# Second products of scores and key bits contracted over the rows in use, and no clearing of the other rows, in a fused LSH attention and two-layer MoE kernel

## The chip, the cores and the metric

The kernel runs on one core of a Trainium2 chip. The metric is the device time of one execution in microseconds (us). Five engines work side by side: TensorE (PE, with its weight loads shown apart as PEld), VectorE (DVE), ScalarE (ACT), GpSimd (POOL) and SyncE (SP), which here only issues DMAs. Each engine runs its instructions in the order in which they were written for it.

## What is computed

```python
q_bits = (einsum('bhsd,dk->bhsk', q, proj) > 0)      # 6 bits per row, B=2 H=8 S=768 D=64
k_bits = (einsum('bhsd,dk->bhsk', k, proj) > 0)
mask   = bucket(q_bits)[:, :, :, None] == bucket(k_bits)[:, :, None, :]
scores = where(mask, q @ k.T / sqrt(D), -1e9)
attn   = softmax(scores)                             # row sum + 1e-9
x      = (attn @ v) as [1536, 512]
h = x @ w_in;   g = piecewise(h);    x = g @ w_out   # 512 -> 2048 -> 512
h = x @ w_in2;  g = h - tanh(h);     out = g @ w_out2
```

Everything is wanted in float32 accuracy, so nearly every product is made of three: high part by high part, high by low and low by high.

## The kernel before, in words

The attention is cut into 32 groups (batch, pair of heads, half of the queries, head of the pair), and each group into three tiles of 128 queries by 768 keys: 96 tiles. Batch 0 comes first (48 tiles); the matmuls of the two MoE layers of batch 0 are mixed between the tiles of batch 1, and those of batch 1 come at the end, on other, 16-bit parts.

For a group, `prep_q` and `prep_k` split the queries and keys. A key tile has two halves of storage: `a` (128 partitions, high part twice over) and `b_`, in which partitions 0 to 63 hold the low part and partitions 64 to 75 (`R0:RC`, twelve rows) the hash bits of the keys. The queries have `Aq` and `Bq` in the same way. Scores of a tile are two products into one PSUM tile (`emit_s`): `first` contracts `Aq` with `a` over 128 partitions, `second` contracts `Bq` with `b_` over 128 partitions, twice each since the 768 keys are two halves of 384. A mismatch of bits adds a large number, so a minimum over the row (L662) and an exponential (L663) give the softmax.

The bits come from a product too. `first_k` (for the first two heads) and `k_bits` (for all others) make, for each half of 384 keys, two matmuls into the one bank `pb`: `phl_w` with `a`, and `phz` with `b_` (L419, L436), both over 128 partitions. VectorE then compares `pb` with a threshold and writes the twelve bit rows of `b_` (L422, L439). `q_bits` does the same for the queries with other weights (L449, L450, L453).

Partitions 76 to 127 of `b_` and `Bq` are in no use. Since the products run over 128 partitions they must hold zeros: POOL clears two key tiles (L284) and three query tiles (L293) at the start, one DVE memset clears a piece of `phz` (L304), and `prep_k` calls `clear` (L395 to L402) for each of the six other key tiles of batch 0, which live in storage that the MoE uses later. The key tiles of batch 1 reuse the first two, so nothing is cleared there.

The order of all this work is not found by the program while it runs: each operation is entered in a plan with the engines that could do it, and `SCHEDULE` is a packed list that gives the order of all operations and the engine of each (`Plan.unpack`). 64 entries of the plan are fillers (`spin`, L1330): four small matmuls each whose result nobody reads.

Of the kernel before, what the change touches and what calls it, by code (L numbers as in the profile page):

```python
# [23 lines left out]
    "c-rk)X^dUvd4At-|IWVLbMC(1xifQTyLUW`XT~$0@q)+L#s<d;F<>xz0!eAv9B@zqA*3mVqAHM84lxb1P)JLnhEigcAGD;XRU`7F66)_rRi*yupQ>uw12*<7"  # L24
    "_l`{h5>ow2ckY~XzvbPY=Y7A=00ELK{?1w9oCEqc1@nKt_VVICzANOB5lfL5if_C@NQ#Bw3ml1!fg~tU4y2!Ck_-OCtpQei>zT8HB>VIjo;X2O#!Nu~p(#9c"
    "H@WxVknJHjECU*=$_3|h$KMrlyGP3R-Yc?bPv()ajEr;5rbI~Qg5e4v5~O*lPY<0I>e8L;CU23mJ$!Bf0SPERH@6iRcfj}p1t6bnqdj{W9I#+{`ikA=vWYkL"
    "<Dk{X1=^1iw+&RVJYD7W*;2EPwNkAFg%adTBLIs-t;%37J3Ct}<=X8+!5YSNI#V1QX$@ssne>1Ww_$8-Y$R&MgK?<>&8VPK;g+xxUK_@RMm4U5g~C{51%+&w"
    "d+(FUgqSzIY#vYLa+xUOrZDvY6kq;?@-3@sWy?_|lL3=z-v~fO@N~njyWeFtSiqco{xRnX%PLwHp;>1cxk#JvyV1*c2>m4&P1~g2gl8jphA`qPt}IKPkN`JU"
    "QYru6{urdsge%13dl=qt*vz!p<xJkSP2z67br}}g_u-Z;WKrlvs)kyVM`rj87jWg39Y`EVk&^?a&7Nz0o0#9c)a1r9`wr}@a~1y~{m!00C{yt@@i^kcVvaqy"
    "z`yiWHot|y)O}wjTE9xh2_?txwcF&*J6|M!KKwaKDIvmo&JyI7r%u+mCj5HA9_Noe^c499d4iDNNA?JN8-MZeL44yO_SRSMp(~I)@aARW0r3j{@2@%D|C3Yf"  # L30
    "$3OlXln%mO|9PkWcU%Gu&pvzoZNCEf+}kIm1MoxZouMCmAO7X%C%$+1djKZBj{2!nn!ZN0rmraLuYUHrGU-qL3t92kIQt`-f05>L&%ellJx3A^AEVJTt{?98"
    "e{~oAHhkxo@BA`&`|V&XLI^#>r10jO|N0Ma>0kV_P3i_AipV&AgTT*TMMTGYjR3`0_)pEdj1U>Zi!Ld^^DYDXS<auKCr_TVjn7yo@Ptm30nT$;FFuy@v*^Vv"
    "k{~QW4f>F6T8`s{4twPI7wqHSOlSw?;O>ClX3)<IMY%)y*ZJWTKYFbZa5m_%{gPd0-@;r9G(qY%!zIo^pv#hN7TUxeWM^JG4zYLHwz3Y*DRW}_)`?F|9HKWE"
    "$xvdcQ93fxCY`MvI=^jxNV#fj|K`nfc9x5onYz|f)k$NSl-1be9yL}TEpalWXK_UJDLSz<7;mn3GOW_rd_>Upe0m~1SQseKE1GgV>WmL{cI;?`G;C!08e1xr"
    "TBbT}c_Lk)ol-nSGZO{dZn=Y+sA#mGT+)a2`E6lPpABki&ex-|Fh1NVmxG2e(irvqD;kxoQI)QdiJVl_?}RxVEMm1;;O;c?$$rKLW1FR`+blL?`tBC9gyTqp"
    "$)k2wTsLmklyx|0Uuic(Lfiv&&*YBQR=6B8COs`vCKh?j4P&#MPN##yCRb}22vZFyt{1H|<wl*(gqeB0Wh$6_-7FMM9fpUp7BYEYaCk7<+oDu1D<R!#^?}$t"
    "?vSOWV`$#9RW01HAm?5A4QKk+>0AFO{dE=DH*TVTuNC7*9)9?X?kSWnk;6){;7|2^{uln~Pjp_oPyhU_yP31k{JZbkru>mE3Q(`zkb70(TT+VX(Z6`(FO8IC"
    "h}RDr`jpOyXKmZg*)M!0dw*6~U<%RaUE=+<?eWa*H`*_&*fw5LW+wRNpP8`&tsU*1^7P+IcFdNZP{vP{4onR%xyw&j&ubxnc=Mxb``zjXdg*>wM^uT=GWH}t"
    "#vEp!ypdVof0S#k_3i#u`bqZSx4tEWWh-IY_uqFtKYEm3_i)vGh;up2B|bRDIm>#i?!vLXG)3_aeC&30+vl;F|BU?P&9^99+=5>oxZX6y@nc7iAitN$;4bNW"
    "8g1kOvis0IAn(ahNlVurp`d@y`E>X@oTR14Zs2^`u3wfEk|~)0<Fh*{qIVPB->00t*FtE|UbRdBb{fX^@D97exHmtbHnE$*F3@X_`e2S<eRUrrap5qtfDQsn"  # L40
    "*va1CmSgSqUNSbe-AA4t8p7J_owF)RxNyc<c6JHmJJb!OQNzYzsW!<Sdb=@g95U>Ka=$dQ3IbW&y>)rlXe2&0EVAywLoSWe4$M#<R(zWB!VJxlB|@$cxdWkj"
    "v~$hX`#K#}QpH-Vt)R4|gH}-3TaZm3^iCMjY|#o9l<&HI?tU{3me}OSozUEtTB3f?G8~wl%}Gbi&`EP@!5oscrP`6JY}YsRoPBWi69plfEj^LlGi42BEYUIN"
    "%7(83p%f{#+g?%`YBj-a1y0Lz28!<Wg)!;W!Oobr4Fxp}N(iCsg0gB+Suhsl%iO_CJ8wE8x?`u%>JTOQNMpM)mi)!RKEL5_617f^lgouzwq$W|hb$DA%A0v("
    "xG_;0V9kRE+q|03=XVb6;H<nWE;Sd*t-h-c=CNLY%L)f4NtD|kRd!WiCq{X{oe%x~m{Pp09!-%ZX$1adCE|r6*PyvvxNTQbC31(1n{;}9UwTU;iu?Ndrgp>_"
    "ZOW))y1k{ayikafXu=e12NA^mm$zpR4#=@D;+_#}FB=-4bo}ZzbCj`b9Ou%J;YDYQ-mK@Ke>yYWmr)(nR(sl)LMqi6Nq4T?K9rV&a{KNh3(EtoDUc%A)f8f4"
    "OzabjrYMb$8s-e*P`jNQRtjeZT1`DR(9{i`s_S7(6DZYMNvQ#z%Vl$%vM7$za3D+flK%emZpg;<u$EBL!X^H~Yzo4C#jR5d(}Vz`H9fs`W}yu*AHjIiQPqNx"
    ">Tm#N?2U!_sqw!4z5&u8MeWxMWs<8CxwTmVUCE~7Vq7d0a!YYBmm9G(#*m5nGSOt*mrAj6TaJp6mhZcxZi^+Z8w{O#8KO#5XXSi47o{L$I_b0-$NM6WhF%c#"
    "kN9q1z3y4_RnT=SE)|O<8nxRc4RSOyGpsTyHf3tqXw*|uw)`MarRr{ZN&ONjwJw+>tx|JQCKV+FE2KHKsWaK>2;UgRQQI-O*)mEXl~F4t$}3&06rF-%32dYx"
    "BQGaaBU#U3t|+mBQQ#ViTE*$u4FW#TZ9%2WsXbvjR?-QLQz@EEByNrdQgMljTAAi4%jZMaqmdWs8M{esYp71CYuQcTsvBq-m8wxnn`VK;EH{=RL0ZbeWH{%("
    "?enBED{9$!+Xw=dBANzD1yLY(GV0UNQIjSkv!>A|wWN_Qmy#AaX=X`Zj>nQyPHCC=9*GJGxjB}dYN0bQFz8sO=hf>LRBJW2!pmiDdKw^M-8jel1qTu+%PrS^"  # L50
    "m$-Qlm{2`Wx+m~t()~Cbu>d5eAW4$sL&av`Q^|KK$&#eh!7v75a2Q>}`jW1=X?o_BWku|Qw5)7VW-=zRmj`Sx9D;7uQ2c$V%DK8sLD7`|?F(-rX9*1{`X9b2"
    "JItqyS(d|07^F#OuB+K(YsP4*l%kL)B|<XAAWiIaWQy1`TsLV+h|MHeRmU<=8~wVRfFkb_#TarLg;p52EoIKQNhsP5MU#{akdVVH2qkz_6lKP8kkot+NDA!G"
    "noQXcSf(R}pkocXMk^_6jYfY%*P-6$S-M=OIm+|gk=a}(n>aLbSST%7XReXx;w71o1B9Z4D4m2(#nb>d>7fz_C!HNln!$b`nWSZfupC0bec#W6mrbU`c3_7o"
    "@HSyG!I&_T6OC&R^xMT&KiEdYs%DKwxuQ!9O2w#<ph)F%(n!-GKZ$C;fua_<)Cq!OkT(sBo4ItHg($HKI3cs13kCv}1`g=a#04=#f`%+eamW(CNN7ZeDU!&m"
    "K>JO{%BhNzDVc5oWR6;eETl8OOnet6{$^-XYJv;NAuqv?<S1Agy@YrucqFN!iJeK>AiBtsUO8!BDTu^+#snmRg|mWSpA}dk1XjFy_W`;IS@C!ELN;`nL)Ncw"
    "ZkHZgtRKB{;Ho(nus~NGJ|w}9Xzcl>UHHp)-{Nnp!^d3kBXa$3D~4fwcx(0ef7O!#7v-XSTu^sWE+)jqbh{`Q<>M^med!Lhi?I9uO6IsG_P9D7$VZVHxGv|&"
    "*)M$WPNZ8-;;PZf6TuD6fA~Ra%egJdnS&JhfHi83No2$G+ls^5ihT&4i^&?jV4bnBE^uq!pZj^E1LFrhQ=Qg=thN?cMg@BwOUVTtY~PP<53_y))>@NJ>)nD~"
    "R>h5O7VwPoaN|hy&=c4BbM*#YgN_$s^9O?}Suu&My*xPgg5YXEU~e2F_P|bW2b>*@U1Eb5Y*?=?Pb-f-VS~7#p65-rwV@}c>5KHh?73+KdniqMQY5ZbVl9V|"
    "b(?gVaoW#hrT*B14iPsd&0YkuY74|w>TCea)wA*Z-abRJq*t)8H;C7(LV6&hy93BN=0NPqdbpNqx?j|t$y4m^GhD+G2&;nF1((>1<FR*D=;k1@zF^=+1$4FR"
# [1320 lines left out]
```

## Time and profile before

| | us |
|---|---|
| three runs, median | 725.91 |
| lowest and highest of them | 722.04, 726.06 |
| the profiled execution | 722.02 |
| its span (first to last instruction) | 720.2 |
| around the span | 1.8 |

The profile is that of the fourth execution, which is 3.9 us below the median of the three. Every row in this document comes from it. PE and PEld are busy times whose ends are modelled, so a share near 100% says that matmuls follow one another, not that each is as fast as can be. The chain of work is followed back from the last instruction: at each step to what released it, or to the instruction before it on its engine.

### The profile page before, as it was taken

What the parts mean: (1) busy time and instruction counts of PE and PEld (TensorE: products, weight loads), DVE (VectorE), ACT (ScalarE), POOL (GpSimd) and SP (SyncE); (2) the same over time, 40 slices, a digit from 0 to 9 for tenths busy, and PEclk for the clock granted to TensorE, in tenths of its full rate; (3) what the DMA queues carried; (4) which work ended last, traced back from release to release, by engine and by line L of the source; (5) the groups of instructions that cost most, each with busy time, mean ns of one, the idle gap of its engine ahead of it and who ended that gap; (6) DMA issues with size and microseconds to landing.
All of it is one profiled execution on the core that took longest, in us unless ns stands there. A gap on an engine that the chain in (4) does not pass through costs nothing.

```text
span 720.2 us, 12689 instructions
## 1 busy us (share of the span) xinstructions
PE 698.8 (97%) x4516; PEld 558.1 (77%) x4516; DVE 645.4 (90%) x973; ACT 506.3 (70%) x852; POOL 464.4 (64%) x383
## 2 busy tenths in 40 slices
...
GB/s 238 209 219 303 250 303 291 232 214 247 259 250 259 214 277 229 188 255 253 186 182 227 230 256 155 196 118 82 107 63 103 59 78 28 100 59 88 45 45 87
DMA packets 168655, 129.45 MB, mean 180 GB/s; under 512 B 127840, under 2 KB 138640, under 8 KB 168592
## 3 DMA queue, kind: packets, MB, share of 16 engines
...
## 4 chain that ended last, share of the span: by engine, by line
PE 75%; DVE 16%; issue 3%; DMA 3%; ACT 2%; POOL 0%; SPq 0%; DVEq 0%; ACTq 0%
PE mm L1043 44%; PE sbk L1076 8%; PE pv L1076 4%; PE pv L771 3%; PE ss L644 3%; PE ss L648 3%; DVE smt L662 3%; PE pb L1076 2%; PE pv L761 2%; DMA pt<-phl 1%; DVE phl L668 1%; PE sbk L1031 1%; DMA krs<-in_kT 1%; DVE wr L941 1%; PE mm L731 1%
## 5 line engine op out<-in xcount | busy, mean ns | idle before, releaser
L1043 PEld LDWEIGHTS <-late_w 128*128 128x128 f16 x720 | 70.4, 98 | 48.8 <-issue 2.2
L663 ACT ACTIVATE p<-ss,smt 128x768 f32<-128x768 f32 x78 | 70.1, 898 | 53.9 <-DVE smt L662 52.1
L670 POOL TENSOR_TENSOR phl<-p,phl 128x768 f16<-128x768 f32 x44 | 77.0, 1750 | 40.3 <-ACT phl L668 15.2
L662 DVE TENSOR_REDUCE smt<-ss 128x1 f32<-128x770 f32 x82 | 78.3, 955 | 15.1 <-PE ss L648 12.9
L1043 PE MATMUL mm<-late_gh,late_w 128*128 128x384 f16 x368 | 85.5, 326 | 2.0 <-DVE accs L1168 2.0
L963 POOL TENSOR_TENSOR wl<-wr,wh 128x512 fp32r<-128x512 f32 x49 | 69.6, 1427 | 25.4 <-DVE wh L961 11.3
L1076 PEld LDWEIGHTS <-late_w 128*128 128x128 f16 x528 | 51.1, 98 | 35.4 <-issue 2.4
L1043 PE MATMUL mm<-xh,wh 128*128 128x384 f32 x256 | 72.1, 342 | 1.8 <-DVE tmp L1145 1.7
L1043 PE MATMUL mm<-gh,wh 128*128 128x384 f32 x256 | 72.5, 343 | 0.6 <-DVE accs L1179 0.6
L1043 PE MATMUL mm<-xh,wl 128*128 128x384 f32 x256 | 70.7, 337 | 0.0
L1043 PE MATMUL mm<-gh,wl 128*128 128x384 f32 x256 | 70.6, 336 | 0.0
L1043 PE MATMUL mm<-xl,wh 128*128 128x384 f32 x256 | 70.5, 336 | 0.0
L1043 PE MATMUL mm<-gl,wh 128*128 128x384 f32 x256 | 70.4, 336 | 0.0
L963 POOL TENSOR_TENSOR late_w<-wr,late_w 128x512 f16<-128x512 f32 x34 | 46.1, 1360 | 14.8 <-ACT late_w L961 12.5
L962 POOL CAST wh<-wr 128x512 fp32r<-128x512 f32 x34 | 26.9, 795 | 38.1 <-PE mm L1043 22.1
L1043 PEld LDWEIGHTS mm<-xh,wh 128*128 128x128 f32 x256 | 46.3, 188 | 5.2 <-DVE tmp L1145 2.4
L941 DVE SCALAR_TENSOR_TENSOR wr<-w,wr 128x512 int32<-128x512 int32 x64 | 49.3, 782 | 1.0 <-ACT wr L939 0.2
L1043 PEld LDWEIGHTS mm<-gh,wh 128*128 128x128 f32 x256 | 46.3, 188 | 2.7 <-issue 1.7
L1043 PEld LDWEIGHTS mm<-xh,wl 128*128 128x128 f32 x256 | 46.9, 188 | 0.0
L1043 PEld LDWEIGHTS mm<-gh,wl 128*128 128x128 f32 x256 | 46.8, 188 | 0.0
L1043 PEld LDWEIGHTS mm<-xl,wh 128*128 128x128 f32 x256 | 46.8, 188 | 0.0
L1043 PEld LDWEIGHTS mm<-gl,wh 128*128 128x128 f32 x256 | 46.7, 188 | 0.0
...
## 6 DMA issues: line engine op xcount, KB each, us to landing
...
```

Source lines behind the costliest of these rows:

```text
L644: T.matmul(ps[:, c, 0:SH], Aq[n][:, i * 128:(i + 1) * 128], a[:, c * SH:(c + 1) * SH], start=True, stop=False)
L648: T.matmul(ps[:, c, 0:SH], Bq[n][:, i * 128:(i + 1) * 128], b_[:, c * SH:(c + 1) * SH], start=False, stop=True)
L662: one("V", 870.0, lambda: V.tensor_reduce(z, sx, axis=AX.XY, op=ALU.min), cell, [c])
L663: one("A", 880.0, lambda: A.activation(halves(p), s, AF.Exp, bias=z, scale=-1.0, accum_out=LS[lm][:, lk:lk + 1]), cell + [c], pc + [("ls", ...
L670: lo = [("G", 1600.0, lambda: G.tensor_tensor(hl[:, S:2 * S], p, hl[:, 0:S], op=ALU.subtract)), ("V", 870.0, lambda: V.tensor_tensor(hl[:, ...
L761: T.matmul(ps[j * 64:j * 64 + 64], f[:, kc, j, :], pt[j][:, kc, 0:SH + 1], start=kc == 0, stop=kc == KC - 1)
L771: T.matmul(ps[j * 64:j * 64 + 64], v[:, kc, a, j, :], PT[n[j]][:, c * KC + kc, 0:SH + 1], start=(kc == 0 and i == 0), stop=(kc == KC - 1 a ...
L941: one("V", 600.0, lambda: V.scalar_tensor_tensor(wi, yi, 3, wi, op0=ALU.logical_shift_left, op1=ALU.bitwise_or), [("w64", i, 0)], [("wr", ...
L962: ("G", 580.0, lambda: G.tensor_copy(whl(n)[0], WR[r]))], [("wr", r)], [("wh", n)])
L963: op([("G", 1225.0, lambda: G.tensor_tensor(whl(n)[1], WR[r], full(whl(n)[0]), op=ALU.subtract)), ("V", 600.0, lambda: V.tensor_tensor(whl ...
L1043: T.matmul(ps[:, s + hf, 0:SH], m[:, kc * 128:(kc + 1) * 128], y[:, hf * SH:(hf + 1) * SH], start=(kc == 0 and i == 0), stop=(kc == 3 and ...
L1076: T.matmul(sbk(n), m[:, sl], v, start=(j == 0 and i == 0), stop=(j == 1 and i == 2))
```

## The change

The second product of the scores runs over 76 partitions in place of 128 (`Bq[n][0:RC]`, `b_[0:RC]`), and the second product of the keys' bits over 64 (`phz[0:R0]`, `b_[0:R0]`). All the clearing is gone: the memsets at L284, L293 and L304, the function `clear` and its six calls. The bits' product is no longer entered as a reader of the bit rows. `SCHEDULE` is packed anew. Unpacked as `Plan.unpack` does it, the list has 3,614 operations in place of 3,620: the six clears (four on ACT, two on POOL) are gone, all others but the fillers stand in the old order and on the old engines, and four of the 64 fillers stand later, from within the first 206 places of the list to places 211 to 213 and 995.

```diff
-    for m in range(2):
-        G.memset(Bk[m][R0:].bitcast(F32), 0.0)
...
-    for z in Bq:
-        G.memset(z[R0:].bitcast(F32), 0.0)
...
-    V.memset(phz[64:128, R0:RC].bitcast(F32), 0.0)
...
         a, b_, ac, bc = kt(g)
-        if b == 0:
-            clear(b_, bc[1:3])
         m2 = kcount[b, hp, j] % len(kr)
...
-    def clear(t, cells):
-
-        n = t.shape[-1]
-        src = warm[R0:].unsqueeze(1).to_broadcast([R0, n // 128, 128])
-        dst = t[R0:].rearrange("p (a b) -> p a b", b=128)
-        op([("A", 100.0 + n * 0.82, lambda: A.activation(dst, src, AF.Copy, scale=0.0)),
-            ("V", 60.0 + n * 1.04, lambda: V.memset(t[R0:].bitcast(F32), 0.0), 1),
-            ("G", 60.0 + n * 0.8, lambda: G.memset(t[R0:].bitcast(F32), 0.0))], [], cells)
...
                 T.matmul(ps, phl_w, a[:, cols], start=True, stop=False)
-                T.matmul(ps, phz, b_[:, cols], start=False, stop=True)
-
-            one("PE", 350.0, mk, [ac[c], lo] + bc[1 + c:2 + c], ["pb"])
+                T.matmul(ps, phz[0:R0], b_[0:R0, cols], start=False, stop=True)
+
+            one("PE", 350.0, mk, [ac[c], lo], ["pb"])
...
                 T.matmul(ps, phl_w, a[:, cols], start=True, stop=False)
-                T.matmul(ps, phz, b_[:, cols], start=False, stop=True)
-
-            one("PE", 350.0, mk, ac + bc[0:1] + bc[1 + c:2 + c], ["pb"])
+                T.matmul(ps, phz[0:R0], b_[0:R0, cols], start=False, stop=True)
+
+            one("PE", 350.0, mk, ac + bc[0:1], ["pb"])
...
-                T.matmul(ps[:, c, 0:SH], Bq[n][:, i * 128:(i + 1) * 128], b_[:, c * SH:(c + 1) * SH], start=False, stop=True)
+                T.matmul(ps[:, c, 0:SH], Bq[n][0:RC, i * 128:(i + 1) * 128], b_[0:RC, c * SH:(c + 1) * SH], start=False, stop=True)
```

## Rows read from the trace of the kernel before

**Rows 1.** The page: busy time of each engine, share of the span, instructions.

```profile
PE 698.8 (97%) x4516; PEld 558.1 (77%) x4516; DVE 645.4 (90%) x973; ACT 506.3 (70%) x852; POOL 464.4 (64%) x383
```

**Rows 2.** The page: the chain that ended last, by engine.

```profile
PE 75%; DVE 16%; issue 3%; DMA 3%; ACT 2%; POOL 0%; SPq 0%; DVEq 0%; ACTq 0%
```

**Rows 3.** Busy time by stretch: us, PE, PEld, DVE, ACT, POOL, PEclk, DMA share, GB/s.

```profile
24.00:48.00 24.00, 19.89 (x159) 14.59 (x160) 22.68 (x36) 19.48 (x34) 19.13 (x14) 1.00 1.06 226
156.00:286.00 130.00, 129.34 (x808) 122.51 (x807) 119.99 (x177) 97.31 (x164) 83.00 (x67) 1.00 1.00 247
```

**Rows 4.** The chain in order of time, first 75 us: start, us, what.

```profile
8.24 0.43 POOL xl L402
...
19.36 0.44 PE pb L435
...
61.43 0.18 PE pb L435
```

**Rows 5.** The chain in order of time, from 150 us on.

```profile
173.16 0.18 PE pb L435
...
388.47 3.15 PE mm L1043 x18
...
397.54 0.18 PE pb L435
...
528.57 2.92 PE mm L1043 x18
```

**Rows 6.** Clears by line: count, ns (min/median/max), first and last start, form.

```profile
L284 POOL MEMSET bk<- x2: 732/732/733, 0.7 to 1.4; 64x768 f32 x2
L304 DVE MEMSET pw<- x1: 68/68/68, 3.3 to 3.3; 64x12 f32 x1
L400 ACT ACTIVATE xl<-warm x3: 840/840/844, 7.8 to 34.5; 64x768 fp32r<-64x768 f16 x3
L402 POOL MEMSET gl<- x1: 738/738/738, 39.2 to 39.2; 64x768 f32 x1
```

**Rows 7.** Timeline around the clears: start, us, engine, instruction [idle before, releaser].

```profile
5.88 0.99 POOL L340 TENSOR_TENSOR bk<-krs,ak 64x384 fp32r<-64x384 f32 x1 [2.60 <-ACT ak L331]
...
34.49 0.84 ACT L400 ACTIVATE xl<-warm 64x768 fp32r<-64x768 f16 x1
...
36.80 0.90 ACT L663 ACTIVATE p<-mm,smt 128x768 f32<-128x768 f32 x1 [0.45 <-DVE smt L662]
...
41.29 0.19 PEld L449 LDWEIGHTS pb<-ab,pw 128*128 128x128 f32 x1 [0.31 <-POOL ab L340]
```

**Rows 8.** Timeline of PE around a group of matmuls with 64 output columns.

```profile
119.32 0.34 PE L1043 MATMUL mm<-gh,wl 128*128 128x384 f32 x1
119.58 0.88 PE L708 MATMUL pb<-unit,ls 128*64 128x128 f32 x12
120.39 0.44 PE L1043 MATMUL mm<-xh,wh 128*128 128x384 f32 x1
120.67 0.34 PE L1043 MATMUL mm<-xl,wh 128*128 128x384 f32 x1
```

**Rows 9.** Timeline of PEld and PE around a transpose of six columns.

```profile
229.20 0.08 PEld L695 LDWEIGHTS pb<-unit,ls 128*6 128x6 f32 x1
...
229.38 0.27 PE L695 MATMUL pb<-unit,ls 128*6 128x128 f32 x1
229.40 0.59 PE L1043 MATMUL mm<-xh,wh 128*128 128x384 f32 x2
```

**Rows 10.** By line: weight loads of 6 and of 128 columns.

```profile
L695 PEld LDWEIGHTS pb<-unit,ls x8: 81/82/83, 210.0 to 458.9; 128*6 128x6 f32 x8
L648 PEld LDWEIGHTS ss<-bk,ab x112: 186/188/190, 10.7 to 455.6; 128*128 128x128 f32 x112
```

**Rows 11.** Groups by form, first 75 us: form, count | busy us, mean ns | idle.

```profile
L331 ACT ACTIVATE ab<-qr,cb 128x384 fp32r<-128x384 f32 x7 | 4.2, 607 | 0.0
L331 ACT ACTIVATE ab<-qr,cb 64x384 fp32r<-64x384 f32 x2 | 1.2, 608 | 0.0
```

More of the change, by code (lines that the diff above doesn't have):

```diff
@@ L23 @@
 SCHEDULE = (
[L24 to L59, printed above, removed]
@@ L60 @@
-    "HZXl%@{m>QknVt7Q+QUafn9#>Ma`=U?Hcc_ia@vC2)iYD_q4^|=ti2nd%2H*D|$1;(+PqrttRJZdt7PK1r$$Qm2~G}+tZyAcJc6;77h_M>Orul{qL<n&ev^`"
-    "(}+Rn#S}<Z1MK{@gj`@TC94eW5$4_-_U26NmU-**83DTob6q*=+Tw4VE@x8a!fG#`W4H}-3(sW(;@O^J^*Y!Cr?`>l&L9rgyQHVG@5gLy-8q}I>)=b^gBQVd"
-    "dY(B=;rp05|7nD5ylWSaeYo;}XN2W7"
+    "c-rk)X^dUvd4At-|IWVLbMAKTy>qu&?ristXYq_ZV~-a+#x^!~oDc&B0|64#lopeiB`AToX;Wf?qJ%6&gqQ|e8c0i`hEigMAGD-MRU=ZVQq<p(s!ILQAFV2-"
+    "JzyKpa_`tAL5)<u(#)MX_x--_U7z>)jsXHBr~IET2<IHow<(zadFs1wye;I^h^5H0$&U#MSrBj}7)XKw<zV(pOme|b-w|M+Z#{iMkmSel$tS7GnHdNmG=+!m"
@@ new lines @@
+    "gnJJT+a7|$a-gxQTyXBX?`<K+JyJe#Lgdk&EFfc98ReTzi2y!;;RqlSq_Nwh2hRz0=ni(9yM^uMn-&m|fa04r&EwV`FtI>kYHA9|;WpZH`(VEXGY5B@OC}EB"
+    "kk!ToI)D<l4fbJWrpoJc<^DR>%C#~iWhj<M0k#ge`i2Vmxw%rg&~7J*HG<h}t~5T{8qT$H*+C<2!}$34Xw-^_;&LDKM~TXWo5Q~FrZ7$#)wmWW$#`T1Nj@yR"
+    "^OMVkSTwzS5ziJ1xhUsmF!K<UUiyIYEvstfD^XuA2PW0N5rB%|>4sf*pJX;zz?@?7wDY)Sl`M<Uyt9N{WKH<J=%u@b{<MpxZBlR2vynVQ7;zO>mZhGO0JrsJ"
+    "GXB4Q38c@2E5u`a7(QUw%(U3GOrF>#akt*G1Pkr^ar0)fRp_l$4Y#I_&hl9<;JWKN@WD1x<m7;9v*%i0C+1hLHo5W4z61N}T*Y6Y-`MlV6)OHvJcf8mY+?^D"
@@ new lines @@
+    "@K65%o8L@e`u@)ltzRJ%gpvn8X}8He_q;&9JMue}QbL6FoF&K|Pn@Z7P53Q>J;qNz@&x%Zd7O|xLiRcK7XI|qA$<K2_U32tk%LGcdgB`Lka!vY=a(EG_`zBB"
+    "{qO$`N(bS@f83-04HrSfv(Mgg{1+gfd+UsJ0KQ}WeE8enf`9(WQ{O!DO#l;LL;b{AO<$#2)0dU?S3i19ne+$$g{<^TockUvzCa6w=U?E!o+GJ+r)l(z>xX;&"
+    "U!0&{hj0As=RXVHdMg-@5JJx|DZKH<zx@51`ltVBle$5OA~KF&C-9?J5Yh2oB|!0I{zLPG5h6o)!6gYi?=rBT<@_0X=FAz}_^9<1KBZG*fb)XZTTd7KJbE#U"
+    "BnV4TgFa%Lmg6{~!#?-mefERiY-k6S;NE~9H|WQOqTHeU^ZZDLAG^s2I2-cVe#vgO?_e$knl|Y+!zIokpi7c%6xzfcWM@&2I}WjT*|xF{Z&K#u%$<`TnmkNz"
@@ new lines @@
+    "HBwz-sWCb_+9sVX9Xh{leptC`%fQBsbZ(A|+1a|*)72?siB#11)E+fn87p%#tmkl4H5Hv)9EvyAJ2}?Z*mzXX_I!3SJCqD2^kBc7h&mI)ogF(GAq^Y3W@B?-"
+    "UoBUiu{@DYXr~-c)7)fY+bwrU6BUgOkgJ+lpWhY+^|_#?Hu-u?CKDr_N+oC*qm41&KiKHY8&&BVxyZ>x15Q}Lp%Pa66YkC+pBi9nD7IO)y3Jy<rtfYx%Q%4~"
+    "m^x<X#my6DO<6~R_H}lDNQir&?wQ=t+6tFK#-yiZ#>5hjxnXRSGudpAY;d)ffiTsu;(Du<rQE2~*)TV+H%|vsubD~7)M0oyZy}QhhDL^>y)8=Rk`mIbRv(JZ"
+    "2OYAwcoNM|Y*7n$FUWaUe%YD1bLP%3W<ReY`?d}A@3dn4=&4hma?hfCksMKq1%ImV_wW0MKhZ_$KK+w7?`6(D^KYNDP5C`t5};naweX6<H>DKOqkr-GUm6+9"
@@ new lines @@
+    "5U(9E^jVz~&)T+Ku>btC`3LgC0#k^lca`_ow#RdK-Dba}V%vC8nYrMre`dxCw05+2*3&<h?4&I{p^P6Y9he$kbeA5tp4UQt=k`a{_IuU0_2L7rj;InJW9%#Z"
+    "By*U3<~C-1>rt+`)_3{W>#wkfzxFjDEL#cFe&GIF__1UB=2KPk5zgfZm-z5F=Pd8Bx(g@w(hSAB@$_Bl_{Xuo_)+=6+wV}exC1{kc#CO@2TvY5iu{vA1}CKR"
+    "VYHD4$nHn?fc!*(N?N|@C<Xod&WFR_<s>UTb}Q#gcKw=kl1$6AGd{MHB6=U8`<u$ydlQ8A-1SQYV5ebh5AU}7829D})dqGu*a^Mqm=ET}4L39yiIXGD0y+dN"
+    "g(rJ|TaLHed&&6tb{~0mco=JQ_spp%1;bfq$=M~4?@+gv#|#@sq}m{N=<UXgaoDgA$^FvID+pw1_m-tyW0CmKh{(H#4!bnYIxtIl*yq!X7v^Z5ED~~16b^*u"
@@ new lines @@
+    "vCfS*?CW$?S(R$Bwu17a4q8F7H<A55=$$aC*;Xr9P`>Ln-Th`3EV03lJE6HPvq=4*WjHW5SCEdHrBmkgf;lW}i?yTI+pcfuP4=O=4<thLxAbIw&$Kn1vqZ<-"
+    "R55%N2&G85-S*PaP^$@UD{xw#GgxwONyep92RmolHY92Uln_GMiLz=@MKBf=E8M|cyJ$M2x?^Y1>JTOQXk)uF7X7V5O~2u95VcN?lWT=ovSev!hfGR~m5sbH"
+    "(wHm{vi?Jd+PqpU7IzNs;H<JMF841~TFvVZ6|tVcHOZkV5*7AGeY^T#Cq_lTT@3w!m{L4mkETgKX$1Z?W#WaSH=?<e9N(3WiNayyBRV_3FT1%B#m#1OdPj`W"
+    "hMYR7+nbZ6g(Ob13DdA0L=X>L+nzf#D91mAdq%CjY<ObI@vGa+F~)9moU2DiwmO^jM!g9JW^yyloa(5y+S9%oGMUb3wsYO~;jA2z+jk#bSQ>0igA~E8ejz5u"
@@ new lines @@
+    "#Xhms6y>oo!<<DNZnp~~O5yBat6z@~_Uneu)b)s^36yKCbk+bb6!Ha5Sro@vIFP4%$-qE%H{|1bSW6*k;VOS&E(77d(w6Ck8A1Tjnwi-$yU+%hk6<FDRJCBV"
+    "Iud{xd*fkodZIbd93%}=(tbUukV2ivE&Y9<`|{bi6qm|LVKFWh3Zs_B7;;fF7fr>@Oomn3a!ic2eBT{&TPzLTQ0UYv5cNfMRw-r+Q3i6Rlg*lOyf5--=mo*R"
+    "sP8uGb<diwg05R}xl}6CsNF7WkYl;o5tUQ1DKjHRqn?qn<p+T(S9i;+>Q_mrbz+jN%4~{qnJ5KVA<gLxovBVo_{JEH*^bH0mQe<&j9NK0Ug=U_$w?GT+eR8P"
+    "@(NNl()}FfiZV-#gli~i6=!2NWu^1n7F4>N+LNYZrBrBwO3}|m8s=y)6PKx|RcMj2Vli|*8hMePwfm`U4c94kExX^h>IPayU)3mQO*0`eD~#tzkd<;MRp;Ed"
```

13 lines of the change are left out of this document (added).

## The prediction

> **What bounds the kernel now.** I read the page first: PE is busy 698.8 of 720.2 us, DVE 645.4, the others far less [rows 1]. The chain that ended last says the same: 75% PE, 16% DVE [rows 2]. A share is an average, so the next view is the stretches. From 24 to 48 us DVE has 22.7 of 24 us of work and PE 19.9: there PE waits for DVE. From 156 to 286 us PE has 129.3 of 130 [rows 3]. So a microsecond saved on ACT, POOL or DVE in the early part counts only if DVE's queue gets shorter, and one added to PE after about 45 us counts almost everywhere. The granted clock is 1.00 in both stretches [rows 3], the upper of TensorE's two levels; the change leaves the number of matmuls as it is, so I leave the clock out.
>
> In the PE part the pace is set by the weight loads: 18 matmuls of 32-bit parts took 3.15 us, 175 ns each, 18 of the 16-bit parts 2.92 us, 162 ns each, both with 384 columns [rows 5]. The load of a 32-bit part takes 188 ns [rows 10] and runs while the matmul before it streams.
>
> **The clearing that goes.** Four clears on ACT of 0.84 us are 3.4 us; two on POOL and the two of the key tiles at the start are 0.73 each, 2.9 us; the three query tiles are half that size, by estimate 0.37 each, 1.1 us; one DVE memset is 0.07 us [rows 6], where of a line with several tiles one stands and the others are as long. In all 7.5 us of three engines. What lies over it:
>
> At the start POOL, done with its memsets by 3.3 us, sat idle 2.60 us until ACT had split the first keys at 5.88 [rows 7]. The keys' DMA is the cover, and the DVE memset lies under it too. Gain 0. Without that cover it would be the 2.5 us of POOL.
>
> On ACT, the clear at 34.49 has an exponential behind it, and the one after that waits 0.45 us for DVE's minimum at 36.80 all the same [rows 7]. What the clear gives back, ACT spends waiting for DVE, which is full [rows 3]. The two before it, from 7.8 us on [rows 6], lie in the stretch in which the keys still arrive; the fourth is like that at 34.49. Gain 0; all four exposed would be 3.4 us.
>
> On POOL, the clear at 39.2 stands ahead of the subtraction for which a weight load of the queries' bits waits 0.31 us at 41.29 [rows 7]; at most that is won there. The other one, at 8.24, has 0.43 us on the chain [rows 4]; but it lasts 0.73, to 8.97, and the chain leaves it at 8.67, so it did not release what came next. Gain 0, at most 0.7.
>
> So I take 0 for the clears, with 7.5 us as the bound of all of them exposed and about 1 us as the most that the waits show.
>
> **The fillers.** Twelve small matmuls of 128 columns took 0.8 us [rows 8]; the four fillers that move are sixteen of about that size, so about 1.1 us of PE, which is taken from the head and given back later. The bounds are 1.1 us either way; I take 0, since PE waits in both places for others and a filler uses up waiting. No wait is added: the bits' product only loses a reader's entry, and its place stays.
>
> **The second product of the scores, over 76 rows.** Nothing in the trace contracts over fewer than 128 partitions. The nearest rows on the number of partitions are ACT's: the same operation took 607 ns on 128 and 608 on 64 [rows 11]. On PE the load goes with columns: 82 ns for 6, 188 for 128 [rows 10], and here the columns stay 128. So a matmul over 76 rows costs what it cost: 0. The bounds: if the shorter load let these 192 matmuls go at the 16-bit pace, 13 ns each, 2.5 us less; if the array must be emptied ahead of and behind each of the 96 pairs, as below, 96 x 0.38 = 36 us more.
>
> **The second product of the bits, over 64 rows.** There are 16 key tiles with two halves, so 32 such matmuls, each alone between a matmul over 128 rows and another. Here the trace has a near relative: matmuls with 64 output columns, which use half of the array the other way. Around them PE loses time. The last full matmul starts at 119.32, the first narrow one at 119.58: 0.26 us in place of 0.175, so 0.085 lost; the next weight load was not made ahead. Behind the group the first full matmul starts at 120.39 and the second 0.28 later, not 0.175: 0.105 lost, since the first load lay bare [rows 8]. A lone 64-row matmul would pay this on both sides: 0.085 + 0.105 going in, 0.105 + 0.085 coming out, 0.38 us a visit.
>
> The other relative says nothing is lost: the transpose with six columns had its weights loaded at 229.20, ahead of its start at 229.38, and the next matmul starts 0.02 later [rows 9]. I take the first, since it is an ordinary matmul with half an array's 64, and the second a transpose; the bounds are 0 and 0.38 a visit.
>
> A rule of the Trainium skill bears on this. The page TensorEngine Tiling (Array Packing), section Tiling Modes, counts a contraction over 64 rows as a tiling of its own (two tiles of 64 rows), none for 76, and says that changing the tiling mode, not merely the tile, drains TensorE. The 64-column rows agree with it, the six-column ones do not look like a change of mode. By that rule the sum is the one below; by the six-column row alone it would be 722.0.
>
> **The sum.** How many visits lie on the path? The chain holds the bits' matmuls of the keys (L435 and L436 together) six times in the head, the first at 19.36 and the last at 61.43 [rows 4], and nine times from 173.16 to 397.54 [rows 5]: 15 of 32. The other 17 are not in it: the chain passes them on DVE or a DMA, and between 24 and 48 us the bits' comparison would have to wait in DVE's full queue anyway [rows 3]. 15 x 0.38 = 5.7 us more on PE, nothing back from the clears: 720.2 + 5.7 = 725.9 of span, and with 1.8 us around it 727.7. That stands against the profiled execution's 722.0. The runs shown lie at 722.04, 725.91 and 726.06, so two of the four known times are 3.9 us higher; I add half of that, 1.9, and predict 729.6 us. The ratio that I forecast is 727.7 / 722.0, 0.8% slower.
>
> **Rivals.**
> 1. No drain: 64 rows are handled as the six-column transpose was. Then nothing is paid and the clears give back 0 to 1 us: 721 to 722, on the median's scale up to 726. For it: rows 9. Against it: rows 8 are the closer form. Chance 0.20.
> 2. Faster. The weight load gets shorter with its rows, and PE runs at the load's pace where the change acts. Of 192 + 32 matmuls, at 13 ns each, 2.9 us, and with 1 us from the clears 718; it ends over 1% faster only if the clears come free too (7.5 us, 711.6). It decides as soon as a 76-row load falls under the 162 ns of streaming. Against it: ACT's 607 and 608 ns, and loads that go with columns. Chance 0.08, half of it beyond 1%.
> 3. The 76-row product drains as well: 96 more visits at 0.38; with the share 15 of 32 on the path, 17 us, with all of them 36: 745 to 764. For it: 76 is not 128 either. Chance 0.07.
> 4. Every one of the 32 visits is exposed, since a late bit comparison delays DVE where DVE is full: 32 x 0.38 = 12.2, 734.2, with the 1.9 us 736. For it: L439 follows L436 in each case. Chance 0.05.
>
> **How the numbers follow.** My forecast has 0.60. A measurement of this kernel can tell about 1%, 7.2 us, from no change. The forecast gives 5.7; it passes 7.2 if 19 visits count, or a visit costs 0.48: I give that a fifth, 0.12. Slower: 0.12 + 0.07 + 0.05 = 0.24. Faster: 0.04. Same: 0.72. The range goes from 720, where rival 1 ends, to 737, where rival 4 ends; it leaves out rival 3 and the far half of rival 2.
>
> **What would show it.** Right: the matmul of L436's line has its weight load begin only when L435's matmul is through, PE starts 0.26 us apart in place of 0.175 there, and the matmul behind it is late as well; the score's second product keeps 175 ns; the ACT and POOL clears are gone and the waits for DVE behind them are longer. Wrong: starts 0.175 apart around L436's line (rival 1); loads of 76 rows under 188 ns (rival 2); gaps around the score's second product (rival 3); DVE's comparison L439 waiting for PE in most of its 32 runs (rival 4). If DVE's work from 24 to 48 us ends earlier, my zero for the clears is wrong.

## The result and the profile after

| | before | after |
|---|---|---|
| median of six runs, us | 725.98 | 733.17 |
| lowest and highest | 722.04, 727.63 | 732.91, 733.89 |
| the profiled execution, us | 722.02 | 733.25 |
| its span, us | 720.2 | 731.5 |

The changed kernel is slower: the ratio of its times to those of the kernel before is 1.011, with a 95% interval from 1.0083 to 1.0137, which leaves out 1. The medians are 7.2 us apart, 0.99%; 1.1% would be 8.0 us. 729.6 us was predicted, from 720 to 737. The spans of the two profiled executions are 11.3 us apart, more than the medians, because the one of before was among its shortest; sums below go by medians where they can.

Busy time by engine and the chain by engine, from the page of the changed kernel (to [rows 1] and [rows 2]):

```profile
PE 712.9 (97%) x4516; PEld 561.8 (77%) x4516; DVE 646.6 (88%) x972; ACT 502.5 (69%) x848; POOL 458.3 (63%) x376
PE 82%; DVE 10%; DMA 2%; ACT 2%; issue 2%; POOL 0%; SPq 0%; DVEq 0%; ACTq 0%; POOLq 0%
```

ACT has 3.8 us less to do and POOL 6.1; the clears that are gone make up 3.4 and 4.0 of that [rows 6]. PE has 14.1 us more for as many matmuls, and the chain lies on PE for 82% of the span where it was 75%.

The line of the bits' second product in the changed kernel (L420; before L436): count, ns (minimum, median, maximum), first and last start, form, for the 16 of its 28 instructions that lie in batch 1; then, for all 28, what the weight loader PEld waited for ahead of them and who waited for them:

```profile
L420 PEld LDWEIGHTS pb<-bk,pw x16: 182/183/183, 161.6 to 406.3; 64*128 64x128 f32 x16
L420 PE MATMUL pb<-bk,pw x16: 435/436/443, 161.6 to 406.3; 64*128 64x384 f32 x16
...
  issue: 6.2, 28
who waited for it (us, times):
  DVE bk L423: 2.4, 5
  DVE gl L423: 0.9, 1
```

Ahead of all 28 (the other four of the 32 are in `first_k`, L403) the loader sits idle, 0.22 us each, released by nothing that the profile shows ("issue"). In the kernel before, nothing sat idle ahead of L436. The load of 64 rows takes 183 ns, the load of 128 rows took 188 [rows 10].

One visit in a stretch where PE is full, timeline of PE and of PEld:

```profile
226.95 0.34 PE L419 MATMUL pb<-ak,pw 128*128 128x384 f32 x1
227.22 0.44 PE L420 MATMUL pb<-bk,pw 64*128 64x384 f32 x1
227.59 0.62 PE L1027 MATMUL mm<-xh,wh 128*128 128x384 f32 x2
...
226.78 0.19 PEld L419 LDWEIGHTS pb<-ak,pw 128*128 128x128 f32 x1
227.22 0.18 PEld L420 LDWEIGHTS pb<-bk,pw 64*128 64x128 f32 x1 [0.25 <-issue]
227.59 0.30 PEld L1027 LDWEIGHTS mm<-xh,wh 128*128 128x128 f32 x2 [0.18 <-issue]
227.87 0.36 PEld L1027 LDWEIGHTS mm<-xl,wh 128*128 128x128 f32 x2
```

The loads tell the story. The load ahead of L419 runs at 226.78, under the matmul before it. The load of L420 does not start at 226.97, when the loader is free, but at 227.22, as L420 itself does; the load behind it again starts bare, at 227.59. The row of 227.59 holds two matmuls; the second starts at 227.87, with the load that follows. So the starts are 0.27, 0.37 and 0.28 us apart (226.95, 227.22, 227.59, 227.87): 0.92 us for three steps that take 3 x 0.175 = 0.525 elsewhere. This visit costs 0.40 us. Over the 16 visits from 150 us on, the three steps take 0.915 us in the median, and 0.524 around L436 in the kernel before: 0.39.

The chain of the changed kernel in order of time, start, us, what: visits of L420, the first and the last among them, and a stretch with scores:

```profile
31.51 0.37 PE pb L420
...
227.29 0.37 PE pb L420
...
233.13 0.36 PE ss L632 x2
...
236.77 0.35 PE ss L628 x2
...
406.37 0.37 PE pb L420
```

The second products of the scores over 76 rows (L632) take 0.36 us for two, as the first ones over 128 rows do (L628, 0.35): no gap like that of the bits. (A few nanoseconds a pair come up below, with e13 and e14.) The 64-row matmuls stand 23 times in this chain, 10 times up to 65.75 us (one of them as L403) and 13 times from 161.69 on; the bits' matmuls stood 15 times in the chain before [rows 4, 5].

### The profile page after: what moved, and what is told of

The parts are those of the page before. It is cut to its first block, busy times and chain, and to the rows that moved or that the text cites. A ratio compares the mean times of both kernels' runs of the same rounds, so it can differ in the third digit from the quotient of the medians.

```text
span 731.5 us, 12671 instructions
## 1 busy us (share of the span) xinstructions
PE 712.9 (97%) x4516; PEld 561.8 (77%) x4516; DVE 646.6 (88%) x972; ACT 502.5 (69%) x848; POOL 458.3 (63%) x376
## 4 chain that ended last, share of the span: by engine, by line
PE 82%; DVE 10%; DMA 2%; ACT 2%; issue 2%; POOL 0%; SPq 0%; DVEq 0%; ACTq 0%; POOLq 0%
PE mm L1027 48%; PE sbk L1060 7%; PE pv L755 4%; PE ss L628 4%; PE pv L1060 3%; PE ss L632 3%; PE pb L1060 2%; PE pv L745 2%; DMA pt<-phl 1%; PE pb L420 1%; DVE smt L646 1%; PE sbk L1015 1%; PE mm L715 1%; DMA krs<-in_kT 1%; PE pv L1314 1%
## 5 line engine op out<-in xcount | busy, mean ns | idle before, releaser
L946 POOL CAST wh<-wr 128x512 fp32r<-128x512 f32 x34 | 26.6, 787 | 41.8 <-PE mm L1027 22.7
```

Source lines behind the costliest of these rows:

```text
L946: ("G", 580.0, lambda: G.tensor_copy(whl(n)[0], WR[r]))], [("wr", r)], [("wh", n)])
```

## The experiments

Each kernel was run together with the kernel before, on the same chip; the ratio is to those runs, with its 95% interval.

### Which of the two products costs (e1, e2, e3)

e1 is the kernel before with the bits' second product alone over 64 rows:

```diff
-                T.matmul(ps, phz, b_[:, cols], start=False, stop=True)
+                T.matmul(ps, phz[0:R0], b_[0:R0, cols], start=False, stop=True)
```

> The kernel before with one edit: the second product of the keys' bits runs over 64 rows; all clears, the order and the fillers are those of before. Theory A (the 64-row matmul empties the array on both sides, 0.40 us a visit in the trace of the changed kernel, and this is the whole change): 6 to 10 us slower than before, ratio 1.008 to 1.013, with PE starts 0.27 and 0.37 us apart around line 436. Theory B (a part of the loss comes from TensorE's clock falling to 1.2 GHz in the head, because four fillers were moved out of it): about 2 us less than the changed kernel, ratio 1.006 to 1.008, and the granted clock stays 1.00 from 0 to 48 us. Theory C (the score product over 76 rows costs): within 0.3% of before.

Measured: 732.25 us, ratio 1.0107 [1.0082, 1.0133]. That is the whole loss of the change, with all clears in place, as theory A had it. The granted clock is 0.86 from 24 to 48 us, so it falls in the head with the fillers in their old places too; theory B had 1.00.

e2 is the kernel before with the scores' second product alone over 76 rows:

```diff
-                T.matmul(ps[:, c, 0:SH], Bq[n][:, i * 128:(i + 1) * 128], b_[:, c * SH:(c + 1) * SH], start=False, stop=True)
+                T.matmul(ps[:, c, 0:SH], Bq[n][0:RC, i * 128:(i + 1) * 128], b_[0:RC, c * SH:(c + 1) * SH], start=False, stop=True)
```

> The kernel before with one edit: the scores' second product runs over 76 rows. Theory A: same as before within 0.2%, matmuls of line 648 still 175 ns apart. Theory C (76 rows cost on their own): some of the 1.1% shows here, at least 0.4%. If fewer rows made weight loads or streaming shorter: 2 to 3 us faster and loads under 188 ns.

Measured: 726.4 us, ratio 1.0029 [1.0005, 1.0054]. Small, but not nothing, and between what theory A (0.2% at most) and theory C (0.4% at least) had said; what it is follows further down (e13, e14).

e3 is the changed kernel with the bits over 76 rows as well. The keys' low part is written over 76 partitions, so that the bit rows hold finite numbers before the bits are there, and the weights have zeros in those rows:

```diff
+    V.memset(phz[64:128, R0:RC].bitcast(F32), 0.0)
...
-        sub_lo(b_[0:64], kr[m2][0:64], a[0:64], 870.0, 1860.0, [("kr", m2)] + ac, [bc[0], bc[3]])
+        sub_lo(b_[0:RC], kr[m2][0:RC], a[0:RC], 870.0, 1860.0, [("kr", m2)] + ac, bc)
...
-                T.matmul(ps, phz[0:R0], b_[0:R0, cols], start=False, stop=True)
+                T.matmul(ps, phz[0:RC], b_[0:RC, cols], start=False, stop=True)
```

> The changed kernel with the bits' second product over 76 rows in place of 64. So that these rows hold numbers, the low part of the keys is written over 76 partitions (the twelve more hold what the weights' zeros take out), and the memset of line 304 is back; no clear, fillers as changed. Theory A: the loss is gone, time within 0.4% of before, PE starts 0.175 us apart at the bits; if the clears had been worth something, faster than before by up to 1%. Theory B: still 2 us slower than before (ratio 1.003) with a clock below 1.00 in the head. Theory C: still 1% slower.

Measured: 726.44 us, ratio 1.0026 [1.001, 1.0043], 6.7 us under the changed kernel by the medians and 6.1 by the ratios. The bits' line in e3's trace, to compare with L420:

```profile
L421 PEld LDWEIGHTS pb<-bk,pw x16: 187/188/191, 159.3 to 400.7; 76*128 76x128 f32 x16
L421 PE MATMUL pb<-bk,pw x16: 334/341/343, 159.5 to 400.9; 76*128 76x384 f32 x16
```

The loader no longer sits idle ahead of it, and the three steps around it take 0.537 us in the median (0.915 with 64 rows, 0.524 with 128). Twelve rows more give back most of the loss. So it isn't fewer rows as such that cost 0.40 us, but the step from a product over 128 rows to one over 64 and back; over 76 it isn't paid. The 0.26% that are left are also what theory B had said for this run (2 us, with a clock below 1.00 in the head: 0.93 from 24 to 48 us), though not by its cause, as e1 and the next run show.

### The fillers (e4)

e4 is the changed kernel with the fillers at their old places; only `SCHEDULE` differs.

```diff
 SCHEDULE = (
...
```

> The changed kernel with the 64 fillers in their old places. Theory A: as slow as the changed kernel, ratio 1.009 to 1.013. Theory B: 2 to 3 us better than it, ratio 1.007 to 1.009, granted clock 1.00 throughout the head.

Measured: 732.97 us, ratio 1.0124 [1.01, 1.0147], the time of the changed kernel, as theory A had it; the granted clock from 24 to 48 us is 0.86. The fillers' move costs and gives nothing that these runs can tell.

### Where the visits count (e6, e7)

e6 has the 64 rows in batch 0 alone (the head, 16 visits), e7 in batch 1 alone (16 visits from 156 us on, `R0` and `RC` of the first line below changed over); the others are over 76 rows as in e3.

```diff
         a, b_, ac, bc = kt(g)
+        rows = RC if groups[g][0] else R0
...
-                T.matmul(ps, phz[0:R0], b_[0:R0, cols], start=False, stop=True)
+                T.matmul(ps, phz[0:rows], b_[0:rows, cols], start=False, stop=True)
```

> The changed kernel with the bits of batch 1 (16 of the 32 products, from 160 us on) over 76 rows, those of batch 0 (the head, to 66 us) still over 64. Theory A (each 64-row product costs 0.40 us of PE, wherever PE is what the others wait for): the 16 later ones are worth 16 x 0.40 = 6.4 us if all count, so this kernel is 4 to 6 us faster than the changed one, near 728. Theory B (the loss is made in the head, by drains there and by the clock that falls to 1.2 GHz when PE runs dry): 0 to 2 us faster than the changed one.

> The changed kernel with the bits' second product over 76 rows in batch 0's sixteen visits and over 64 rows in batch 1's sixteen: the mirror of e6. Theory A (each 64-row visit costs 0.40 us where TensorE is on the path, and e6 showed about half of the loss in the later visits): 13 of the visits that stand on the changed kernel's chain lie here, 3 to 4 us over e3's 726.4, so 729.5 to 730.5, ratio 1.006 to 1.009. Rival (the loss comes of the head alone, through the lower clock there): 726 to 727, ratio 1.002 to 1.004.

Measured: e6 730.05 us, ratio 1.0067 [1.0042, 1.0092]; e7 730.63 us, ratio 1.0086 [1.0061, 1.0111]. With all bits over 76 rows it was 726.44 and 725.97 (e3, e14), with all over 64 it is 733.17. Against these, the sixteen of the head cost 3.0 us by the ratios and 3.6 by the medians, eight or nine visits' worth of 0.40, and the later sixteen 4.5 and 4.7, eleven or twelve; the two together, in the changed kernel, cost 6.1 to 6.7. The prediction counted 6 and 9. The interval of each ratio is 1.8 us wide to either side, so the two halves are not told apart. e6 came out between its theories (3.1 us under the changed kernel, where A had 4 to 6 and B 0 to 2), e7 at the upper end of theory A; its rival, a loss in the head alone, fell.

### Fillers against a lower clock (e10, e11, e12)

In the head of the changed kernel the granted clock falls. Busy time by stretch (columns as in [rows 3]), changed kernel, and below it the two groups of fillers that run then, in PE's timeline:

```profile
15.00:18.00 3.00, 3.00 (x32) 3.00 (x30) 2.71 (x4) 2.82 (x7) 2.99 (x2) 0.50 0.74 219
...
28.50:31.50 3.00, 0.88 (x5) 0.38 (x3) 2.90 (x6) 1.69 (x4) 2.39 (x2) 1.00 1.16 225
31.50:34.50 3.00, 3.00 (x20) 2.51 (x20) 2.91 (x5) 1.74 (x3) 1.65 (x1) 0.57 1.04 201
...
14.53 3.30 PE L1314 MATMUL pv<-warm 128*128 128x112 f16 x36
...
33.19 2.56 PE L1314 MATMUL pv<-warm 128*128 128x112 f16 x28
```

In the stretch from 15 to 18 us the clock is 0.50, TensorE's lower level of 1.2 GHz, and around 33 us it is so again, behind a stretch in which PE was busy 0.88 of 3 us. Before, the 24 us from 24 to 48 had a clock of 1.00 [rows 3]; after, 0.93. The theory was that more fillers ahead of the three waits of the head keep the clock up. e10 is e3, e11 the kernel before and e12 the changed kernel, each with 72 fillers in place of 64. By `SCHEDULE`, 19 of the 72 in e10 and e12 stand where the changed kernel has none (the expectation below says fifteen).

```diff
-SPINS = 64
+SPINS = 72
...
```

> The kernel with the bits over 76 rows and no clears (as in the run with 76-row bits), with 72 fillers in place of 64, fifteen of which stand ahead of three waits of the head (two of them moved there from right behind them). Clock theory: the granted clock stays 1.00 from 0 to 48 us in every run, and the time is 721 to 723, 3 to 4 us less than without. Rival (the fall of the clock costs nothing on the path): 726, as without.

> The kernel before with the same 72 fillers in the same places. Clock theory: 721 to 722 in all runs, 2 to 3 us under the median of before, whose runs lie between 720 and 729. Rival: as before. Against the refilled kernel with 76-row bits and no clears it shows what the clears and the 76 rows are worth at one clock: Theory A says within 1 us.

> The changed kernel with the same 72 fillers. Clock theory together with Theory A: 728 to 730, since the drains stay (7 to 8 us over the refilled kernel before) and the clock's part goes. Rival (the drains alone make 9 us): 733, no better than the changed kernel.

Measured: e10 727.67 us, ratio 1.0047 [1.0026, 1.0069]; e11 725.76 us, ratio 1.0014 [0.9996, 1.0031]; e12 733.48 us, ratio 1.011 [1.0076, 1.0143]. None helps: the theory fell, and each kernel took about the time of its rival or more. In e10's trace the clock falls at another place, from 18 to 24 us, behind three microseconds with PE busy 0.60. But e12 tells the two causes apart: three of its six executions had a mean clock of 0.998 to 1.0 and took 729.85, 731.3 and 731.88 us, while e11's executions at 0.998 to 1.0 took 724.15 to 726.67 with 724.4 in the middle. So about 7 us of loss (731.3 in the middle against 724.4) are there with the clock up; with three executions on one side that is a rough figure.

### Taking the cut of rows back, without the clears (e13, e14)

e13 is the changed kernel with both products over 128 rows again, but still without the clears of the key tiles: the keys' low part is written over all 128 partitions, and the three query tiles are cleared once at the start.

```diff
+    for z in Bq:
+        G.memset(z[R0:].bitcast(F32), 0.0)
...
-        sub_lo(b_[0:64], kr[m2][0:64], a[0:64], 870.0, 1860.0, [("kr", m2)] + ac, [bc[0], bc[3]])
+        sub_lo(b_, kr[m2], a, 870.0, 1860.0, [("kr", m2)] + ac, bc)
...
-                T.matmul(ps[:, c, 0:SH], Bq[n][0:RC, i * 128:(i + 1) * 128], b_[0:RC, c * SH:(c + 1) * SH], start=False, stop=True)
+                T.matmul(ps[:, c, 0:SH], Bq[n][:, i * 128:(i + 1) * 128], b_[:, c * SH:(c + 1) * SH], start=False, stop=True)
```

> The changed kernel without its cut of rows: scores' and bits' second products over all 128 rows again, as before, but still without the clears of the tiles (the keys' low part is written over all 128 partitions, so that the rows behind the 76th hold finite numbers, and the queries' tiles and the weights have zeros there, the queries' cleared once at the start). Theory A (nothing is gained from the clears that went): the time of the kernel before, ratio 0.999 to 1.001. If the fewer rows are what costs e2 and e3 their 0.3%, this stands 2 us under e14 and its mean clock is that of the kernel before (0.997 against 0.993 to 0.995). Rival (the 0.3% comes of the clears that are missing, or of the order around them): the same 726.4 as e14.

e14 is e3 once more, on the chip of e13.

> The kernel of e3 again (scores and bits over 76 rows, no clears), on the chip of e13 for a direct comparison: 726.4, ratio 1.001 to 1.004, mean clock 0.993 to 0.995.

Measured: e13 721.04 us (719.43 to 722.0), ratio 0.9944 [0.9922, 0.9966]; e14 725.97 us, ratio 1.0024 [1.0003, 1.0045]. e13 is faster than the kernel before, which neither theory had expected. Either the clears were worth 4 us after all, or something else moved. The timeline of VectorE at one place, first in the kernel before:

```profile
356.78 1.22 DVE L668 CAST phl<-p 128x768 f16<-128x768 f32 x1
...
359.20 5.01 DVE L668 CAST phl<-p 128x768 f16<-128x768 f32 x1
364.25 0.96 DVE L1145 TENSOR_TENSOR tmp<-mm,tmp 128x768 f32<-128x768 f32 x1
```

then in e13:

```profile
356.68 1.23 DVE L655 CAST phl<-p 128x768 f16<-128x768 f32 x1
...
359.12 1.99 DVE L655 CAST phl<-p 128x768 f16<-128x768 f32 x1
361.14 0.96 DVE L1132 TENSOR_TENSOR tmp<-mm,tmp 128x768 f32<-128x768 f32 x1
```

Up to this cast the two kernels run 0.10 us apart (356.78, 356.68); behind it they are 3.11 us apart (364.25, 361.14). So after 357 us of work all the clears that went had given 0.10 us, and one cast gave 3.0. GpSimd's timeline at the same time, in the kernel before:

```profile
359.11 1.64 POOL L670 TENSOR_TENSOR phl<-p,phl 128x768 f16<-128x768 f32 x1
360.72 1.84 POOL L340 TENSOR_TENSOR gl<-tmp,gh 128x768 fp32r<-128x768 f32 x1
362.52 1.27 POOL L963 TENSOR_TENSOR wl<-wr,wh 128x512 fp32r<-128x512 f32 x1
```

and in e13:

```profile
359.02 1.67 POOL L657 TENSOR_TENSOR phl<-p,phl 128x768 f16<-128x768 f32 x1
360.65 2.16 POOL L338 TENSOR_TENSOR gl<-tmp,gh 128x768 fp32r<-128x768 f32 x1
362.78 1.29 POOL L950 TENSOR_TENSOR wl<-wr,wh 128x512 fp32r<-128x512 f32 x1
```

Before, the cast ends at 364.21, 0.42 us after the third of GpSimd's products. In e13 it ends at 361.11, 0.42 us after the first; it slipped in between the first and the second, and the second took 0.32 us longer. In the traces of the changed kernel, e1, e2, e3 and e14 this cast took 5.02 to 5.03 us. The same cast takes 0.55 us in the median of its 15 places.

The clock differs between e13 and e14 too. Mean granted clock over the executions: 0.9982 in e13, 0.9928 in e14, as in e3, and 0.9972 in the kernel before on that chip. Busy time by stretch, e14:

```profile
15.00:18.00 3.00, 3.00 (x31) 3.00 (x30) 2.40 (x3) 2.66 (x5) 2.92 (x3) 0.50 0.75 207
...
31.50:34.50 3.00, 3.00 (x29) 2.70 (x28) 2.91 (x5) 1.75 (x4) 1.64 (x1) 0.52 1.13 222
```

and e13:

```profile
15.00:18.00 3.00, 1.49 (x14) 0.88 (x11) 2.87 (x5) 2.97 (x7) 3.00 (x2) 1.00 0.71 208
...
31.50:34.50 3.00, 2.34 (x23) 1.96 (x23) 2.97 (x5) 2.41 (x5) 2.84 (x2) 1.00 1.28 140
```

The order of the work is the same in both. VectorE's timeline in e14 at the cast:

```profile
362.05 5.03 DVE L653 CAST phl<-p 128x768 f16<-128x768 f32 x1
...
367.12 0.96 DVE L1130 TENSOR_TENSOR tmp<-mm,tmp 128x768 f32<-128x768 f32 x1
```

e14 begins the cast 2.93 us behind e13 (362.05, 359.12) and ends it 5.98 behind (367.12, 361.14): 2.9 us from the part ahead of it, in which the half clock in the head and the few nanoseconds of the next paragraph are all that I found, and 3.05 from the cast. The medians differ by 4.9.

What the 76 rows cost, 1.7 us (e14) to 2.1 us (e2) by the ratios, has two parts. One is in the matmuls themselves. Over the 50 or 51 pairs of the scores' second products from 150 to 460 us, the four steps from the matmul ahead of a pair to the second one behind it take 712 ns in the median with 76 rows (the changed kernel, e2, e3, e14) and 706 to 707 with 128 (the kernel before, e13, e15); around the first products, over 128 rows, they take 707 in all these traces. 5 ns for each of 96 pairs are 0.5 us, if all count. The other part goes with the lower clock. Beside e2, 14 of 23 executions of the kernel before had a mean clock of 0.997 or more and took 723.1 us in the mean, the other nine 726.2; of e2's twelve only three had it, with 723.8, and the nine others took 727.2. So at either level e2 is 0.7 to 1.0 us slower, on few executions, and the rest, some 1.1 us by estimate, comes of the lower level being more frequent.

### The cast by itself (e15)

The cast was only read off two traces, so the last kernel moves it: the kernel before, clears and all, with this one cast done by ScalarE at the same place in the order. Only one entry of `SCHEDULE` differs; as lists of VectorE's and ScalarE's instructions:

```diff
 L453 TENSOR_SCALAR ab_74<-pb_142,cb 12x384
-L668 CAST phl_94<-p 128x768
 L1145 TENSOR_TENSOR tmp_120<-mm_139,tmp_120 128x768
...
 L961 ACTIVATE wh_105<-wr_101 128x512
+L668 ACTIVATE phl_94<-p 128x768
 L663 ACTIVATE p,ls_91<-ss_146,smt 128x768
```

> The kernel before with one instruction moved, all else in its place: the float16 cast of the probabilities that VectorE starts at 359.20 in the trace before, and that takes 5.01 us there while GpSimd runs three products in a row, is done by ScalarE at the same place in the order. In e13's trace this same cast took 1.99 us and the kernel stood 0.1 us ahead of the kernel before ahead of it and 3.1 us ahead behind it. Theory A (e13's gain is this one stall of VectorE, the clears that went gave nothing): 721 to 722, ratio 0.995 to 0.997, about e13's time, clears and all. Rival (e13's gain comes of the clears): the time of the kernel before, ratio 0.999 to 1.001, and the trace loses the 3 us elsewhere.

Measured: 719.87 us (717.95 to 721.75), ratio 0.9934 [0.9913, 0.9955]. Timeline of ScalarE and VectorE there:

```profile
360.55 0.83 ACT L668 ACTIVATE phl<-p 128x768 f16<-128x768 f32 x1
...
360.17 0.96 DVE L1145 TENSOR_TENSOR tmp<-mm,tmp 128x768 f32<-128x768 f32 x1 [1.07 <-ACT tmp L1144]
```

VectorE's next subtraction starts at 360.17, waiting now for ScalarE's copy, where it started at 364.25. One instruction on another engine is worth 4.6 us, more than theory A had said (721 to 722), and with it the kernel before is faster than with any form of the change but e13, whose interval overlaps with this one. So the stall alone is worth about what e13 gained, with the clears in place. VectorE is 4.1 us ahead at this subtraction (360.17 against 364.25). The lead can be followed on TensorE: the same matmul starts 3.87 us earlier in e15's trace than in that of the kernel before, from 393 us on to 655 us; for e13 it is 3.1 us. Yet the spans end only 2.1 and 1.4 us apart (720.2, 718.1, 718.8). Busy time by stretch shows where 1.7 us go, in the kernel before and in e15:

```profile
660.00:680.00 20.00, 18.00 (x112) 10.71 (x110) 19.14 (x23) 9.84 (x15) 13.45 (x9) 1.00 0.18 59
660.00:680.00 20.00, 17.99 (x101) 10.28 (x100) 18.16 (x24) 9.87 (x14) 13.29 (x11) 0.91 0.13 41
```

The granted clock falls there in e15 and, with the same 0.91, in e13. In the profiled execution of the kernel before it does not; that execution had a mean clock of 1.000 and is one of the shortest, which fits medians that are further apart than the traces.

## Why the prediction came out as it did

**A visit's price: right.** 0.38 us was worked out from the 64-column matmuls [rows 8], 0.39 to 0.40 us was measured, and the rows look as foretold: the load bare, the start of the 64-row matmul 0.27 us behind the one before it (0.26 foretold), the next matmul late as well. The rule of the Trainium skill that was weighed there (TensorEngine Tiling (Array Packing), section Tiling Modes: a change of tiling mode drains TensorE) agrees with the runs on both counts: 64 rows pay, 76 rows don't. The page gives no price; the price here is 0.40 us. That TensorE drains is the page's word; the runs show the loads that are not made ahead and the time that it costs.

**The number of visits on the path: about right, rather low.** I took the 15 that the chain before showed. Against e3 the change costs 6.1 to 6.7 us, 15 to 17 visits; e6 and e7 added up give 7.5 to 8.3 us, 19 to 21; the chain after shows 23, ten in the head and thirteen behind it, where 6 and 9 were counted. How many count is not known better than that. The reason that I gave for the head does not hold: I said that from 24 to 48 us VectorE's full queue would cover the visits [rows 3]. Busy time of the changed kernel in that stretch, to compare with [rows 3]:

```profile
24.00:48.00 24.00, 21.45 (x168) 15.61 (x166) 21.08 (x36) 16.34 (x31) 17.22 (x12) 0.93 1.09 214
```

VectorE is busy 21.1 of those 24 us, not 22.7, and PE 21.5, not 19.9: the visits, and the lower clock, took up the slack that PE had, and VectorE now has slack itself. It does not end earlier for that, which would have spoken against the zero for the clears: the last bits' product of the head stands at 65.75 us in the chain, and at 61.61 in the chain before. VectorE's comparison (L423) waits for PE in 6 of 28 places, so rival 4, with all 32 exposed and 12.2 us, did not come. Rival 1, no drain, fell with the first row of the visit.

**The clears: right at 0.** e1, with the clears, and the changed kernel, without them, lose the same 1.1%, as e2, with them, and e3, without, lose the same 0.3%; each of these comparisons is good to some 2 to 3 us. e13, which keeps the queries' clears, stood 0.10 us ahead of the kernel before after 357 us. ScalarE's exponential waits for VectorE a little longer, as foretold. Groups by line, changed kernel; behind the bar the idle time ahead of these 78 instructions and what ended it, the wait for VectorE's minimum first:

```profile
L647 ACT ACTIVATE p<-ss,smt 128x768 f32<-128x768 f32 x78 | 70.1, 899 | 55.2 <-DVE smt L646 53.4 <-DVE pt L450 1.0 <-DVE scal L501 0.3
```

Before, this wait was 52.1 us. 1.3 us more, in a trace that is 11.3 us longer, fits the forecast but does not prove it.

**The 76 rows: nearly right as to the array, wrong as to the clock.** No visit's price, 5 ns a pair or 0.5 us where I had 0, and the load is no shorter; by line and form, changed kernel:

```profile
L632 PEld LDWEIGHTS ss<-bk,ab 76*128 76x128 f32 x112 | 20.4, 189 | 0.7 <-DVE ab L437 0.7
```

189 ns for 76 rows, 188 for 128 [rows 10], so rivals 2 and 3 fell: 17 us and more for rival 3 stand against 2.1 us of e2, clock and all. But the sentence "the change leaves the number of matmuls as it is, so I leave the clock out" was a step too far: e2, e3 and e14 lose 0.24 to 0.29%, and their mean clock is 0.993 to 0.995 where before it is 0.997. Why fewer rows go with a lower clock stays open. PE's busy time ahead of the fall does not tell the two apart (8.94 of the first 12 us in e14, 9.37 before, 10.01 in e13), and e13 also has three memsets at its start that e14 lacks, though e2 has them and its clock is low.

**The fillers: right at 0**, as far as e4 can tell.

**The median.** I added 1.9 us because two of the four known times lay 3.9 higher than the profiled one. The median of six is 725.98, so 3.9 would have been right here; beside the experiments, with 11 to 23 executions, it is 724.1 to 724.9. 729.6 lies 3.6 under the measured 733.17: 2.0 from this, up to 1.0 from the visits (6.7 for 5.7), and the rest, 0.6 or more, from the 76 rows and the clock, which the sum had at nothing. The forecast of the ratio, 1.008, lies just under the interval measured.
